# A gated mix of a state-space convolution and linear attention: two small steps that may run on either engine, and a newly written-out order

## The chip, the cores and the metric

The kernel runs on one core of a Trainium2 chip. The metric is device time in microseconds of one execution, the median of repeated runs. The seven runs of the kernel before lie between 300.56 and 304.86 us; their median is 302.23 us. The engines that matter here are TensorE (PE in the profile; its weight loads are PEld), VectorE (DVE), ScalarE (ACT) and SyncE (SP), whose instruction queue issues nearly all data transfers (DMAs). GpSimd (POOL) does a few small fills.

## What is computed

The input `x` is 2048 positions of 512 channels in bf16. One branch is a state-space convolution, the other linear attention, and a gate mixes them:

```
g = sigmoid((x * gate_w).sum(-1))
# branch a: state-space convolution, N = 128 states per channel
dt = exp(log_dt);  logdA = dt * (A_re + 1j*A_im);  dB = dt * (B_re + 1j*B_im)
P  = exp(logdA[:, :, None] * l)            # l = 0 .. 2047
K  = einsum("dn,dnl,dn->dl", C, P, dB).real
y  = irfft(rfft(pad(x)) * rfft(pad(K)));   a = y + x * Dskip
# branch b: linear attention, 32 heads of 16
q, k, v = split(xb @ wqkv)                 # xb: the kernel is given x for it
phi(t) = [softmax(t @ w_phi), softmax(-t @ w_phi)]
kv = phi(k)^T v;  z = sum(phi(k));  o = phi(q) kv / (phi(q) z + 1e-6);  b = o @ wo
out = g * a + (1 - g) * b
```

(The reference calls both branches with the same `x`.)

## The kernel before, in words

**Stages.** The start loads `x` as `UD` (four DMAs `ud0` to `ud3` of 512 KB, one per 128 channels, L287 and L1412), builds trigonometric tables for the Fourier steps, and turns the six parameter matrices into the small tables `Ctab` and `Dtab` (prepare, L261). For that it needs `log_dt` in two shapes, `ldc` (1 KB) and `ld` (128 KB), loaded together by one step, `load_ld` (L284, L1408). `ldc` feeds `dtc = exp(ldc)` on ScalarE (L403), which two VectorE products read (L412); `ld` feeds `exp(ld)` (L429). Meanwhile TensorE transforms `x` (psA at L582 into `XAu`, psB at L226 into `XU`), which goes to DRAM as `XUd`. Then come the keys (`pk`, `Ek`, `Zk`, `vr`, `kvp`) and the queries (`pq`, `Eq`, `bps`).

Woven in between are eight groups h = 0 to 7 of 64 channels for the convolution kernel `K` (kgen, L991). Each has two chunks c = 0, 1. For a chunk, ScalarE writes a table `E` (two exponentials) and a table `cs` (cosine and sine), VectorE multiplies them (r_neg L1010, r_pos L1013) and changes the sign of one quarter of the result, `R[:, 1, 0]` (L1014). VectorE also makes `A` (two products at L1005, in groups 4 to 7 a sum at L1018). TensorE multiplies `A` by the table (kps, L213). Sines and exponentials lie in different ScalarE tables, so the sines come in batches of four chunks between two table loads. Four groups of 128, 128, 128 and 64 channels run through `transform` (psB, the product with `U` at L1139, psz, a trip through DRAM as `Zd`, psy). The gate product `o` or `ZA` (ou, L1205) reads psy and is stored. The last 64 channels take `finish` (L1217), which stays on the chip.

Most results of TensorE are copied out of PSUM by `evict` (L554), a step that may run on ScalarE (`nc.scalar.copy`, L563) or on VectorE (`nc.vector.tensor_copy`, L561).

**The order is written out by hand.** Every step is a node added to `Plan` (L92) with an engine, a cost in us and its dependencies. `Plan.run` takes the nodes in the order of the string `ORDER` (two digits per node, base 64), takes the engine of each free step from `SIDES` (0 or 1) and the PSUM pool from `RINGS`. The costs and the `move` value of a DMA are only notes that the order was made with; nothing at run time reads them. What they change is the order. Each engine runs its own instructions strictly in that order: a step that waits holds up all behind it on its engine. SyncE's queue issues the DMAs in that order too.

Tiles are scarce: four `E`, four `cs` and three `A` buffers, one `KD`, two pools of PSUM of two tiles each for this work. A step that takes one waits for the last reader of the buffer's earlier use.

Of the kernel before, what the change touches and what calls it, by code (L numbers as in the profile page):

```python
# [10 lines left out]
ACT = mybir.ActivationFunctionType  # L11
ALU = mybir.AluOpType
# [79 lines left out]
class Plan:  # L92
# [3 lines left out]
    ORDER = ("000n0L0O0M0P0Q0R0N0-0_100S0T0U0k0l0h0105110206080e0i0V0W1217180X131419151a0Y0Z0m161b1c03040j1v1r1u1d1j0o1q1k1l0p1x1e1f"  # L96
             "1w1g1N0b0c091R0v0a0f070y0g0d2E2G1Q1s1m1n1t1h1T2I1M1A2K2F1P1z1B1C1F2J1O2H2M2O2Q2L2N1D1E1G2P2S2T1H1I2R2U2W2V2Y2X1J2-301L"
             "1W1U312_2Z1S3234331y1V1X361Y351Z38393a3b3c3d3e3g3f3h3i3k1i3j1K1-1_20213l3m3n22232824293o3q3p2a25370w0x3r3s3u0q0r2y2c2b"
             "262g3t3w3v2d2e2h2i2f3x3y0s0t3z0u2B3A3C2C2j2k2l3D3Q3R0z2p2m2q2r3B1o1p2o272t2n2v0C2s0D0E2u0F3E0G0H0A0B3F0I0J3S3T0K3G2z2A"
             "2w2x4647452D4c4f484d4g3K3L3H3I3J3N3O3P494e4r3M4u4j4h4s4i3U643V4n4v4k4o4p8S3Y4l4t4w8T8U3Z3W4y428W8V433X3_9U9V404x4C984D"  # L100
             "4z4A4m4E4q4a994G4J4B8X4H4F4b8Y4V4K8Z4I4L9da34N4W4Y4O4M444Z4P8-4X4R508_4-4S92934T9a94909b4Q9f955455914U5896519g979u4_9C"
             "529c9e599D569p5b5f535j9E9n5a9h5c9F5k575g9i5d5e5n5o5q9q9j9k9l9m5h5u9W9G5i9v5l5m9I9o5r9H5v5y5z5C9r5p5s5F9s5t5D5w5A9J5x5E"
             "9t5B5R5G5H9K5U5S5T5V5W5I5J5N9w5K5L5Y5O5P9x605Z5X9y9O61a49P5-9L5M9z5Q5_62639QaY9M9R9N9S65669A679TaZ9B686a696b6cbgbh6daW"
             "6e6f6g9X9Yb19ZaXa56h6j6la66i6k6ma76n6o9-9_bobpa03-a1a8a26W6pah6q6Yaia9a-aeapaqbbb2a_6r6s6tar6uaa6v6Zb0bq6Xab6-b3bcafbr"
             "b4ag70b56w6x6_b9b66y71baaj6z6Aacb76C6Bb8bebsbt6D6Ead72736Fasbdat6G6H74bf6K75bubv7677bibj6L78ak6McI6I6JcJ797a6Nalaubw7b"
             "6ObxambA7fbBancOcKcPcLcQcM6Q6P7c7dbGbC7g7hao7e7j6R7k7lbycRbH7ibD6Sbz6TbE7n7o6Ubk7zbmbl6V7BbFbnav7Aaw7p7DbJaxbIbRcSbSay"
             "d07CbKazbL7E7m7F7GcN7q41d6aAaDbTbUcZcT7HcU7rbM7IbV7J7K7L7tc0bNbWbXbO7M7N7Oc-d3c_cb7P7Q7U7v7Vc1bP7R7S7s7u7x7w7Wd4d5aBaC"
             "cc8cbY7yaEc3d7bZb-8db_c2bQc48ec57T7Y8f8g8h8icVcWc6dvdw8j8k7Zdxcec77X8l8081d1cXcf8m8n8ocd8pcgc8cY7-7_d2d8d9chcidadcdbex"
             "aFey8283aMaNdddy8q8rdJdzdAc9dKdedfcj8485dgdhcaez86dG8sdidjdk88dldBckeDeE8a8t8x8y8z8uaO8v8w8B8AeF87cldHdIdL8FdM8CaPaQdC"
             "898Ddm8bdRdSdDdN8G8HdEcmcne08E8IcpdqdOdUdTcodVdPdFdQdW8JdrdXe1eA8KdYeBe2eOdZePd-d_dncqcrds8Le38N8PeGdo8Me48Qe58OeCeHdt"  # L110
             "eI8RaGaJeJaKaHaIe6eKdpfjfkaLfmfnfre7eZe8eLeMe9eNe-e_dueQeafueRf0foaReSeTf1f2cscvebflfveefsctfteffDecedcweUcucxf3aSeVcy"
             "fEfFfpegfqf4fwfxfyf5fzfBfAeWfGfCfHfIfOfJfLaTeXczeYcDf6f7ehekelemcEaUaVfMfKfNeiejfPfQf8fbencFf9fRfSfTfVeoepfUcAfafWfcfd"
             "cGcHeqercBcCesfXfYfeeteuevffewfZf-fgfhf_g0fig1")
    SIDES = ("0010101010000101100000001100000000100101110100000011000000101000001101110000101001100010100100000100001010000001000000"
             "0000001010111")
    RINGS = ("0111001010110010010000000000000000100022222222222222222222222222222222000002222222222222222222222222222222200000000000"
             "00000000000000000000300000000000000000000000300000000000003000000030300000000330333033")
# [143 lines left out]
def prepare(P, tc, nc, g, evict, psum):  # L261
# [24 lines left out]
    for dj in range(4):  # L286
        P.dma(0.7 if dj < 2 else 3.0, 2.0, lambda dj=dj: g.load_ud(dj), rw=("", f"ud{dj}"), move=2.75)  # L287
# [237 lines left out]
    kp = []  # L525
    for h in range(2):
        box = Bag()
# [284 lines left out]
def queries_and_convolution(P, tc, nc, g, psum, sh, sp, sl, kv, bank, evict):  # L812
# [171 lines left out]
    lastk = []  # L984
# [6 lines left out]
    def kgen(h, T, XA, new):  # L991
# [5 lines left out]
        for cc in range(2):  # L997
# [14 lines left out]
            def r_pos(c=c, cc=cc):  # L1012
                nc.vector.tensor_tensor(out=c.R[:, :, 1], in0=T.E[cc][:, :, 32:64].unsqueeze(1).to_broadcast([128, 2, 32, 32]), in1=c.R[:, :, 1], op=ALU.mult)  # L1013
                nc.vector.tensor_scalar(out=c.R[:, 1, 0], in0=c.R[:, 1, 0], scalar1=-1.0, scalar2=None, op0=ALU.mult)  # L1014
                T.E[cc] = T.cs[cc] = None

# [11 lines left out]
            r1 = P.add("DVE", 1.65, r_pos, [r0], drop=["E"])  # L1028
# [11 lines left out]
            kps.append(P.add("PE", 2.3 if split else 1.15, kp, w + [a0, a1, r0, r1] + T.nc + T.nE + kps + lastk, take=([psq] if cc == 0 and not sep else []) + (["KD"] if cc == 0 else []),  # L1040
# [54 lines left out]
    def transform(XA, ready, Q, off, nd):  # L1095
# [83 lines left out]
        for j0 in range(0, 16, nj):  # L1179
# [21 lines left out]
            def ou(j0=j0, box=box, ok=ok):  # L1201
                gb = g.gT[:, j0:j0 + nj]
                if not ok:
                    box.o = g.fpool.tile([128, nj, nd], BF16, name="o", tag="o", bufs=3)
                nc.vector.tensor_tensor(out=box.o[:], in0=box.ps[:], in1=gb.unsqueeze(2).to_broadcast([128, nj, nd]), op=ALU.mult)  # L1205
                box.ps = None
# [7 lines left out]
            o = P.add("DVE", 1.22, ou, [y], drop=["psum"])  # L1214
# [326 lines left out]
```

## Time and profile before

| | us |
|---|---|
| median of seven runs | 302.23 (300.56 to 304.86) |
| the profiled execution, whole | 302.23 |
| its span, first to last instruction | 300.4 |
| VectorE busy (366 instructions) | 254.6 (85%) |
| ScalarE busy (302) | 226.1 (75%) |
| TensorE matmul busy (4700) | 220.8 (73%) |
| one product of 128x2048 bf16 on VectorE (L1010, L1013, L1005) | 1.22 |
| sign change, 128x1024 bf16 on VectorE (L1014), 16 times | 0.421 |
| copy 128x1024 f32 from PSUM: ScalarE / VectorE | 1.02 / 1.22 |
| copy 128x512 f32 from PSUM: ScalarE / VectorE | 0.59 to 0.63 / 0.685 |
| gate product 128x1024 on VectorE (L1205) | 1.22 |
| ScalarE exponential or sine, 128x1024 f32 | 1.05 |
| ScalarE, 128x128 f32 (Ln and Exp of `Zk`) | 0.31 to 0.34 |
| ScalarE table load, 11 times | 1.28 each |

The profiled execution is 1.8 us longer than its span: the span runs from the first instruction to the last. In the groups a line is read as: source line, engine, operation, output<-input, shapes, count | busy us, mean ns | idle time of the engine just before these instructions and what ended it. In the order of time (the timeline) a line is: start, duration, engine, line, operation, tiles, and in brackets the idle time before it with its releaser.

### The profile page before, as it was taken

To read this page: it belongs to the slowest core of one execution; us is meant where nothing else is said; L and a number is where in the kernel's file an instruction comes from. 1 tells how busy PE (TensorE), PEld (TensorE's weight loads), DVE (VectorE), ACT (ScalarE), POOL (GpSimd) and SP (SyncE) were. 2 spreads that over 40 slices of the span, in tenths; PEclk is the share of its full clock that TensorE was granted. 3 is DMA by queue.
4 is the path that set the end of the run, shared out by engine and by line. 5 is a ranking of instruction groups with operands and counts; after the bars stand their busy time and mean duration, and the time that the engine had idled before them with its cause. 6 is when DMAs were issued, how large, how long until landed. Compare 5 with 4: busy or idle time off the path is not lost.

```text
span 300.4 us, 10490 instructions
## 1 busy us (share of the span) xinstructions
PE 220.8 (73%) x4700; PEld 132.2 (44%) x4700; DVE 254.6 (85%) x366; ACT 226.1 (75%) x302; POOL 4.6 (2%) x17
## 2 busy tenths in 40 slices
PE   0005666444998698985999789999879999689780
PEld 0005554344343264543356554555544445455560
DVE  7786889997599999998997999999989589886541
ACT  2966989998799999989997889874758885742000
POOL 4000000000000000001000000000000000000000
PEclk9999959975799999998699999999979999999796
DMA  5998788679794000000034216475555693849634
GB/s 105 140 161 134 176 118 132 177 126 384 241 366 149 0 4 2 4 3 4 0 82 145 103 51 175 129 190 179 158 147 138 198 258 72 227 128 244 124 63 71
DMA packets 71452, 39.88 MB, mean 133 GB/s; under 512 B 57200, under 2 KB 63472, under 8 KB 71408
## 3 DMA queue, kind: packets, MB, share of 16 engines
q1 hardware_dynamic: 70352, 38.96, 53.2%
q8 instruction: 36, 0.59, 0.8%
q10 hardware_dynamic: 1056, 0.26, 0.5%
q14 instruction: 8, 0.07, 0.1%
HBM read 24.53 MB, written 14.94 MB: 131 GB/s over the span
## 4 chain that ended last, share of the span: by engine, by line
PE 33%; DVE 25%; ACT 20%; issue 4%; DMA 1%; SPq 1%; ACTq 0%; DVEq 0%
PE bps L963 7%; ACT cs L83 5%; PE kps L213 4%; DVE A L1005 4%; PE pk L700 3%; ACT E L83 2%; PE psz L1151 2%; PE psz L1286 2%; PE psB L1123 2%; ACT Ek L83 2%; DVE cs L1013 2%; ACT XA L563 2%; DVE cs L1010 2%; PE pq L887 2%; DVE Ua L1139 1%
## 5 line engine op out<-in xcount | busy, mean ns | idle before, releaser
L1005 DVE TENSOR_TENSOR A<-Ctab,Dtab 128x2048 bf16<-128x2048 bf16 x32 | 38.7, 1219 | 0.1
L582 PE MATMUL psA<-W,UD 128*64 128x256 bf16 x128 | 12.9, 356 | 27.8 <-DMA UD<-in_A_u_dram 26.0
L83 ACT ACTIVATE E<-args 128x1024 bf16<-128x1024 f32 x32 | 31.1, 1047 | 0.5 <-PE args L778 0.4
L83 ACT ACTIVATE cs<-args 128x1024 bf16<-128x1024 f32 x32 | 30.6, 1049 | 0.0
L963 PE MATMUL bps<-Mw,Eq 128*128 128x512 bf16 x128 | 30.4, 380 | 0.0
L213 PE MATMUL kps<-cs,A 128*32 128x64 bf16 x1536 | 25.9, 224 | 4.4 <-ACT cs L83 1.1
L213 PEld LDWEIGHTS <-A 128*32 128x32 bf16 x1536 | 24.5, 152 | 9.2 <-issue 5.4
L582 PEld LDWEIGHTS <-UD 128*64 128x64 bf16 x128 | 11.2, 203 | 29.3 <-issue 29.3
L1010 DVE TENSOR_TENSOR cs<-E,cs 128x2048 bf16<-128x2048 bf16 x16 | 19.5, 1219 | 2.1 <-ACT cs L83 2.1
L712 DVE TENSOR_REDUCE Zk<-Ek 128x64 f32<-128x1024 bf16 x16 | 18.8, 1211 | 2.3 <-ACT Ek L83 2.3
L1013 DVE TENSOR_TENSOR cs<-E,cs 128x2048 bf16<-128x2048 bf16 x16 | 19.5, 1219 | 0.1
L83 ACT ACTIVATE Ek<-pk 128x512 bf16<-128x512 f32 x32 | 17.2, 610 | 2.3 <-PE pk L700 2.3
L226 PE MATMUL psB<-XAu,TB 64*128 64x128 bf16 x256 | 11.1, 248 | 10.7 <-ACT XU L563 4.1
L963 PEld LDWEIGHTS <-Eq 128*128 128x128 bf16 x128 | 11.5, 97 | 15.7 <-issue 3.4
L700 PE MATMUL pk<-Wkp,xT 128*128 128x512 bf16 x64 | 17.8, 421 | 0.0
L83 ACT ACTIVATE Eq<-pq 128x512 bf16<-128x512 f32 x32 | 16.5, 608 | 1.0 <-PE pq L887 1.0
L732 PE MATMUL vp<-Wv,xT 128*128 128x512 bf16 x64 | 15.8, 380 | 1.1 <-DVE vb L561 1.1
L887 PE MATMUL pq<-xT,Wqp 128*128 128x512 bf16 x64 | 15.9, 382 | 0.0
L226 PEld LDWEIGHTS <-TB 64*128 64x128 bf16 x256 | 9.6, 110 | 12.0 <-issue 10.4
L75 ACT ACT_TABLE_LOAD x11 | 14.1, 1283 | 0.9 <-PEq L1525 0.7
L563 ACT CAST XAu<-psA 128x1024 bf16<-128x1024 f32 x10 | 9.6, 1017 | 4.2 <-PE psA L582 4.2
L1068 PE MATMUL psA<-W,KD 128*128 128x256 bf16 x64 | 10.3, 294 | 2.9 <-ACT cs L83 2.2
(197 smaller groups left out, 476.2 us busy)
## 6 DMA issues: line engine op xcount, KB each, us to landing
XUd<-XUd SPq DMA_DIRECT2D x8, 512.0 KB
Ua<-XUd SPq DMA_DIRECT2D x8, 512.0 KB
Ub<-XUd SPq DMA_DIRECT2D x8, 512.0 KB
aexp<-apd SPq DMA_DIRECT2D x16, 256.0 KB
XUd<-XU SPq DMA_DIRECT2D x8, 384.0 KB
ZB<-Zd SPq DMA_DIRECT2D x10, 256.0 KB
Zd<-Ra SPq DMA_DIRECT2D x9, 256.0 KB
UD<-in_A_u_dram SPq DMA_DIRECT2D x4, 512.0 KB
```

Source lines behind the costliest of these rows:

```text
L83: i = self.nc.scalar.activation(**kw)
L213: nc.tensor.matmul(kps[32 * dj:32 * dj + 32, g4, e, :].rearrange("p (o t) -> p o t", o=2), lhsT=A[q][:, o, :, :, d].rearrange("p a b -> p ...
L226: nc.tensor.matmul(ps[:, e, sl, :], lhsT=fc.TB[rows, r, 1 - ri:3 - ri, :].rearrange("p a b -> p (a b)"), rhs=XA[rows, r, ri, :], start=(ri ...
L582: nc.tensor.matmul(box.ps[64 * e:64 * e + 64, i, :], lhsT=g.UD[:].rearrange("p t (e g) -> p g e t", e=2)[:, gw * h + 4 * g4 + i, e, :], rh ...
L700: nc.tensor.matmul(box.ps[:], lhsT=g.xT[st // 4][:, kt, ss], rhs=g.Wkp[:, kt, :], start=(kt == 0), stop=(kt == 3))
L712: nc.vector.tensor_reduce(out=K.Z[:, u, :, :], in_=K.E[:, u, :, :].rearrange("p g (h f) -> p g h f", f=16), axis=mybir.AxisListType.X, op= ...
L732: nc.tensor.matmul(box.ps[:], lhsT=g.xT[st // 4][:, kt, ss], rhs=g.Wv[:, kt, :], start=(kt == 0), stop=(kt == 3))
L887: nc.tensor.matmul(box.ps[:], lhsT=g.Wqp[:, kt, 128 * m:128 * m + 128], rhs=g.xT[b][:, kt, :], start=(kt == 0), stop=(kt == 3))
L963: nc.tensor.matmul(box.ps[:], lhsT=Q.e[m][:, sg, 128 * i:128 * i + 128], rhs=g.Mw[:, 4 * sg + m, :], start=(k == 0), stop=False, skip_grou ...
L1005: nc.vector.tensor_tensor(out=c.A[q][:].rearrange("p o a b d -> p (o a) b d"), in0=Ct.to_broadcast([128, 8, 8, 32]), in1=Dt.to_broadcast([ ...
L1010: nc.vector.tensor_tensor(out=c.R[:, :, 0], in0=T.E[cc][:, :, 0:32].unsqueeze(1).to_broadcast([128, 2, 32, 32]), in1=c.R[:, :, 1, :, ::-1] ...
L1013: nc.vector.tensor_tensor(out=c.R[:, :, 1], in0=T.E[cc][:, :, 32:64].unsqueeze(1).to_broadcast([128, 2, 32, 32]), in1=c.R[:, :, 1], op=ALU ...
```

## The change

Four things change in the code, and the order with them.

1. The sign change is cut out of `r_pos` into a node of its own, `r_sign`, after `r_neg`, on VectorE or ScalarE. The kps step waits for it too.
2. The gate product of `transform` may run on ScalarE, as one instruction for each 128-wide (or 64-wide) position, with the gate as a per-partition scale.
3. The `move` note of the four `ud` loads is 3.7 instead of 2.75.
4. `ORDER`, `SIDES` and `RINGS` are new.

```diff
-    ORDER = ("000n0L0O0M0P0Q0R0N0-0_100S0T0U0k0l0h0105110206080e0i0V0W1217180X131419151a0Y0Z0m161b1c03040j1v1r1u1d1j0o1q1k1l0p1x1e1f"
...
+    ORDER = ("0L0k0h0i000n0M0O080_0j0e0f0N01040o0-0y090p0l0m0a0P0Q0R10110S0U0V0W0X0T0Y1213170Z14151819161a1b0g05020b030c0d06072E2G1u"
...
-        P.dma(0.7 if dj < 2 else 3.0, 2.0, lambda dj=dj: g.load_ud(dj), rw=("", f"ud{dj}"), move=2.75)
+        P.dma(0.7 if dj < 2 else 3.0, 2.0, lambda dj=dj: g.load_ud(dj), rw=("", f"ud{dj}"), move=3.7)
...
             def r_pos(c=c, cc=cc):
                 nc.vector.tensor_tensor(out=c.R[:, :, 1], in0=T.E[cc][:, :, 32:64].unsqueeze(1).to_broadcast([128, 2, 32, 32]), in1=c.R[:, :, 1], op=ALU.mult)
-                nc.vector.tensor_scalar(out=c.R[:, 1, 0], in0=c.R[:, 1, 0], scalar1=-1.0, scalar2=None, op0=ALU.mult)
                 T.E[cc] = T.cs[cc] = None
+
+            def r_sign(c=c):
+                if c.n.at == "DVE":
+                    nc.vector.tensor_scalar(out=c.R[:, 1, 0], in0=c.R[:, 1, 0], scalar1=-1.0, scalar2=None, op0=ALU.mult)
+                else:
+                    nc.scalar.activation(out=c.R[:, 1, 0], in_=c.R[:, 1, 0], func=ACT.Copy, scale=-1.0)
...
-            r1 = P.add("DVE", 1.65, r_pos, [r0], drop=["E"])
+            r1 = P.add("DVE", 1.22, r_pos, [r0], drop=["E"])
+            rs = c.n = P.add([("DVE", 0.43), ("ACT", 0.97)], 0.43, r_sign, [r0])
...
-                nc.vector.tensor_tensor(out=box.o[:], in0=box.ps[:], in1=gb.unsqueeze(2).to_broadcast([128, nj, nd]), op=ALU.mult)
+                if box.n.at == "DVE":
+                    nc.vector.tensor_tensor(out=box.o[:], in0=box.ps[:], in1=gb.unsqueeze(2).to_broadcast([128, nj, nd]), op=ALU.mult)
+                else:
+                    for j in range(nj):
+                        nc.scalar.activation(out=box.o[:, j], in_=box.ps[:, j], func=ACT.Copy, scale=gb[:, j:j + 1])
...
-            o = P.add("DVE", 1.22, ou, [y], drop=["psum"])
+            o = box.n = P.add([("DVE", 1.22), ("ACT", 2.6 if nd == 128 else 4.4)], 1.22, ou, [y], drop=["psum"])
```

Read out of the strings, the new order and sides are these.

- **Sides.** Sign changes go to ScalarE for (h, c) = (1,1), (3,0), (4,1), (5,0), (7,0), the other eleven stay. Gate products go to ScalarE for the first half of channels 128 to 255 and of channels 256 to 383 (eight instructions of 128x128 each). Of the evictions, 29 move from ScalarE to VectorE (20 of 128x1024, nine of 128x512) and 23 from VectorE to ScalarE (16 and seven). One small copy, `ti2` (two instructions of 128x128), goes to ScalarE. Without the sign changes, by stage: in the start VectorE takes two 128x1024 more on balance; with the keys one 128x1024 more and two 128x512 fewer; from the end of the keys to the last sum of `A` two 128x1024 and two 128x512 more. After that sum it takes two 128x512 more, and one 128x1024, two gate products and `ti2` fewer.
- **SP at the start.** Before: the six turned parameter loads, `ud0`, `load_ld`, `ud1`, `ud3`, `ud2`, `wTq`, the two `pz` writes, the small weights with `Wv`, `wTk`, then the `xT` loads. New: the six, `ud1`, `ud3`, `ud0`, `load_ld`, `ud2`, the small weights with `Wv`, `wTq`, a `pz` write, and the `xT` loads ahead of `wTk`. ScalarE issues its two parameter loads before its first sine instead of after it.
- **VectorE at the start.** Three parameter products that need no `log_dt`, then the products of L412 that do, as before. New: the third product with `nAim` and the two steps at L444 and L445 come ahead of the first eviction of `XAu`; evictions 0, 1, 2 of `XAu` are on VectorE, 3 to 7 on ScalarE (before they alternate); `attention_consts` (L231) comes before the first turn of trigonometry instead of within it.
- **Into the keys.** Before: ScalarE's last copy (`Wkp`), table load, gate exponential, then the first `Ek`. New: table load and the first two `Ek` directly, the gate exponential later.
- **Groups 6 and 7.** Before: the four `E` tables of groups 6 and 7 (G12 to G15) are all made while the products `bps` of the third query block (b = 2) run, and ScalarE loads the sine table after its last copy of that block. New: G12 and G13 are made during b = 1, G14 and G15 at the start of b = 2, and the sine table is loaded before ScalarE copies the third `bps` of that block; the argument product of the last chunk comes before kps of group 6 instead of after it. After the last copy of `bS` VectorE has, up to the last sum of `A`: before, r_pos, two products, r_neg, r_pos, a product, r_neg, two products with `U`, a sum, r_pos, a product, a sum; new, r_pos, two products, a sum, r_pos, two products, two products with `U`, a sum.
- **The end.** In `finish` the second copy of `Xb`/`Xa` is on ScalarE instead of VectorE. The last store-bound psy of channels 256 to 383 comes on TensorE before the second inverse step (L1286) instead of after it. The two copies of `KD` of group 7 are on VectorE.

## The prediction

> **What bounds the kernel now.** I read the busy shares first (VectorE 85%, ScalarE 75%, TensorE 73%), then the chain of waits, which goes through all of them (TensorE 33% of the span, VectorE 25%, ScalarE 20%): no engine alone is the bound. So I asked for the stretches between events of the start, the keys, the queries, the last `bps` and the last sum of `A`. Columns: stretch, length, busy of PE, PEld, DVE, ACT, POOL, clock, DMA share, GB/s.
>
> ```profile
> 27.14:267.69 240.55, 198.20 (x3907) 116.62 (x3904) 219.29 (x294) 205.22 (x278) 1.11 (x2) 0.93 0.49 133
> 27.14:75.30 48.16, 28.03 (x473) 24.36 (x470) 43.27 (x82) 43.82 (x48) 0.16 (x1) 0.80 0.79 180
> 75.30:142.00 66.70, 57.49 (x1272) 29.51 (x1270) 61.80 (x84) 63.35 (x99) 0.95 (x1) 0.96 0.26 86
> 142.00:224.00 82.00, 74.74 (x1468) 42.48 (x1466) 77.15 (x90) 66.40 (x98) 0.00 (x0) 0.94 0.41 121
> 224.00:250.20 26.20, 24.17 (x276) 11.78 (x276) 21.03 (x23) 19.92 (x22) 0.00 (x0) 1.00 0.78 202
> 250.20:267.69 17.49, 13.78 (x424) 8.49 (x423) 16.04 (x17) 11.73 (x14) 0.00 (x0) 1.00 0.53 140
> ```
>
> From the first eviction to the last sum of `A` VectorE idles 240.55 - 219.29 = 21.3 us. With the keys both VectorE and ScalarE are full (93% and 95%), from 142 to 224 VectorE is (94%), from 224 to 250 TensorE (92%), and from 250 to 268 VectorE again (92%). The gaps that matter are single waits, found in VectorE's timeline:
>
> ```profile
> 27.14 1.22 DVE L561 CAST XAu<-psA 128x1024 bf16<-128x1024 f32 x1 [2.90 <-PE psA L582]
> ...
> 240.19 1.23 DVE L561 CAST Xb<-psB 128x1024 bf16<-128x1024 f32 x1 [2.82 <-PE psB L1123]
> ...
> 246.74 1.22 DVE L1010 TENSOR_TENSOR cs<-E,cs 128x2048 bf16<-128x2048 bf16 x1 [0.70 <-ACT cs L83]
> ...
> 259.28 1.22 DVE L1010 TENSOR_TENSOR cs<-E,cs 128x2048 bf16<-128x2048 bf16 x1 [1.38 <-ACT cs L83]
> ```
>
> Last, the transfers of the start: the SP timeline, and the stretches of one microsecond around them.
>
> ```profile
> 8.55 0.75 SPq L1412 DMA_DIRECT2D UD<-in_A_u_dram  x1
> 9.35 1.52 SPq L1408 DMA_DIRECT2D ldc<-in_A_log_dt_dram  x1
> 10.91 0.49 SPq L1409 DMA_DIRECT2D ld<-in_A_log_dt_dram  x1
> 11.45 7.61 SPq L1412 DMA_DIRECT2D UD<-in_A_u_dram  x3
> ```
>
> ```profile
> 11.00:12.00 1.00, 0.00 (x0) 0.00 (x0) 0.96 (x2) 1.00 (x1) 0.00 (x0) 1.00 1.36 218
> 12.00:13.00 1.00, 0.00 (x0) 0.00 (x0) 0.18 (x1) 1.00 (x2) 0.00 (x0) 1.00 1.39 138
> 13.00:14.00 1.00, 0.00 (x0) 0.00 (x0) 0.80 (x2) 1.00 (x2) 0.00 (x0) 1.00 1.01 87
> 14.00:15.00 1.00, 0.00 (x0) 0.00 (x0) 0.66 (x2) 1.00 (x2) 0.00 (x0) 1.00 0.92 182
> ```
>
> The rate falls to 87 GB/s at 13 to 14 us and is back at 182 after. I read the dip as `ldc`'s tiny pieces, passing after `ud0` and before the other three.
>
> **The change part by part.** First the work, by durations of the groups. VectorE's evictions: (20 - 16) x 1.22 + (9 - 7) x 0.685 = +6.3 us. Two gate products less, 2 x 1.22 = -2.4; `ti2` -0.4; five sign changes, 5 x 0.421 = -2.1. Sum +1.3 us. ScalarE: (16 - 20) x 1.02 + (7 - 9) x 0.6 = -5.3, `ti2` +0.6, five signs at about 1.0 (a 128x1024 exponential takes 1.05; ends 0.9 and 1.05) = +5.0, two gate products of eight instructions each. An operation of 128x128 took 0.31 to 0.34 us, and neighbours overlap by about 0.1 (two exponentials of 128x512, 0.61 each, took 1.08): 8 x 0.22 to 8 x 0.34, 1.8 to 2.7, taken as 2.5 for their PSUM reads and strided use, so +5.0. Sum +5.3. Both engines together do 6.6 us more work.
>
> The Trainium skill, "ScalarE: Activation LUTs", Rules for kernel authors, speaks against the change: multiply on VectorE, up to about three times faster in bf16. The rows agree for the sign (0.421 against some 1.0). By the page's estimate, "What ACT_TABLE_LOAD costs", 186 ns + 0.833 ns an element, a sign is 1.04 us, and the sum is the same. The same page, "Table sets", puts copy into every set, so that no table load is added; no run here shows `ACT.Copy` in an ACTIVATE.
>
> *Start to keys.* `load_ld` now stands behind three `ud` loads instead of one. In this trace the four `ud` and `ld` pass from about 10 us to 25.7, with the dip at 12.8 to 14.3, so the last three take (25.7 - 14.3) / 3 = 3.8 each. Behind three, `ldc` lands at 25.7 - 3.8 = 21.9 or so; if transfers don't keep their order, at the old time. The table load ends at 17.3, so `dtc` slips from 17.3 to 22, and VectorE, whose queue has the product of L412 next, stands from about 17.4 to 22.1: 4.7 us. What waits behind it is everything to the first eviction: 412, 415, 416 and the other parameter products, then L444 and L445, about 8.0 us by the strides in the timeline, to 30.2. The first eviction starts there, not at 27.14. It isn't a loss of the full 3 us: the old order had waits of 2.90 here, and 1.2 and 1.1 us near 34 and 41, and had the product with `nAim` and L444, L445 (1.75 us) still to do. Walking both queues on with the old durations, ScalarE's evictions of `XAu` end at 38.5 (old 33.7), the first turn of trigonometry on VectorE at 47.4 (old 50.0, but with six more evictions done and `attention_consts`, 2.2 us, and one copy not done), ScalarE's last copy before the keys near 73.2 plus 1 for waits (old 74.2). There the new order gains: before, the table load ended at 75.5 and the first `Ek` began at 77.0, behind the gate exponential and `pk`; now `pk` runs under the table load, and `Ek` begins near 75.5. Value -1.5 us; ends -5 (`ldc` not late: VectorE's queue is through L445 at 25.5 and free for the first eviction at 27.1, so `XAu` ends some 3.4 earlier than walked, plus the 1.5) and +3.2 (the 4.7 stays, less the 1.5).
>
> *Keys.* ScalarE +1.0 (sign) + 2 x 0.6 - 1.0, VectorE +1.22 - 1.37 - 0.42: half of the sum, as both are full: +0.3, ends -0.6 and +1.2.
>
> *Queries to the last sum.* VectorE: 2 x 1.22 + 2 x 0.685 - 4 x 0.421 = +2.1. Against that, the waits shown at 240, 246.7 and 259.3, together 4.9 us, fall where the old order had sines of groups 6 and 7 not ready. They now come some copies earlier, and the products that read them are queued at that place. After the last `bS` copy VectorE had 17.5 us to the last sum; of the new list ten products at 1.13 (their stride) are 11.3. The difference has to fit before, where TensorE is the bound and VectorE idled 5.2 us. I take 4.2 of the 4.9, as the waits for TensorE itself (0.24 and 0.63) stay and something new will be late: the `bps` chain. Value -2.1; ends -2.8 and +2.1 (nothing recovered).
>
> *After the last sum.* `Xb`'s copy and the product beside it now run on two engines: -1.2 (VectorE's copy lay between two products). The psy put ahead of the second L1286 costs TensorE 1.0 on the path. The two `KD` copies stand behind a gate product on VectorE, 0.1. Value -0.1; ends -1.2 and +1.2. The ScalarE gate products lie where it idles (2.7 and later 27 us free); without that cover each costs 1.3.
>
> Sum: -1.5 + 0.3 - 2.1 - 0.1 = -3.4. The profiled execution is 302.23 whole, equal to the median of the runs, so about **298.8 us**.
>
> The order of passing is also in the skill, "DMA: Bandwidth & Descriptors", Queues, rings and completion order: an engine takes a ring's descriptors in ring order. By it `ldc` is late, which the dip also says.
>
> **The rivals.**
> *The waits move, and the work stays (slower).* Up to the last sum VectorE gets 2.44 (start) - 0.57 (keys) + 2.13 = 4.0 us more work. If it idles 21.3 us there as before, the end comes 4.0 - 0.1 later: 306.1. For it: two of three stretches are over 92% full, and a reordered queue of strict order makes new waits. Against: 4.9 us of the idle time sits in three waits whose cause is moved. It decides from the point where VectorE's idle time between first eviction and last sum stays at about 21 us.
> *The late `ldc` is paid in full (no change).* Then +3.2 instead of -1.5: 302.23 + 3.2 + 0.3 - 2.1 - 0.1 = 303.5. For it: ScalarE's first `Dtab` exponentials wait as well, and from 44 to 74 both engines had few gaps to catch up in.
> *`ldc` isn't late (faster still).* -5 in the start: 295.3. Against it stands the dip.
> *The signs on ScalarE hold up kps.* r_sign follows in ScalarE's queue, and kps waits for it now. Behind r_sign stand the sines or copies, 1 us each. A sign taken at the wrong time is one wait of about 1 us on TensorE; five make +2, 300.8 with the rest as above.
>
> **How the numbers follow.** A difference of under 1%, 3.0 us, is about what a measurement of this kernel can't tell from none. Forecast with the waits filled (about 296 to 299.2) 0.33, `ldc` in time 0.08: faster 0.41. `ldc` paid in full, or signs that hold up, or half of each: 0.27 within 1%. Work stays: 0.32 slower. The likeliest sum is 298.8. The range for 8 in 10 takes the early `ldc` (295.3) with a little, and the slower case with some of the late `ldc` on top: 294.8 to 307.5. That leaves out both ends added up.
>
> **What would show it.** Right: the first `Ek` at 76 or earlier; `dtc` at 21 to 23 and VectorE idle for over 4 us before L412; the three shown waits gone and VectorE's idle time to the last sum near 17 to 18; the last sum to the end about as long as before (32.7 us). Signs at 0.9 to 1.05 and gate instructions at 0.2 to 0.35 on ScalarE, still eleven table loads. Wrong: `dtc` at 17 (the transfer step falls), VectorE idle of 21 or more (the filling falls), or new waits of TensorE on a sign.

## The result, and the profile after

The changed kernel is slower: 306.14 us median (301.69 to 310.45, 27 runs) against 301.93 for the kernel before (299.06 to 306.54, 64 runs). The ratio is 1.0096, with a 95% interval of 1.0071 to 1.0121. It is taken over the faster executions of each kernel alone (for the changed one 15 of 28, those within 1.5% of its fastest), which is why it is smaller than the 1.4% between the medians. The forecast was 298.8 us, faster: the range of 294.8 to 307.5 holds the time, but the sign is wrong. The profiled execution of after took 304.52 us whole, 302.7 in its span, against 302.23 and 300.4 of before.

The events of the prediction (first `Ek`, first step after the keys at L825, last sum of `A`) cut both executions alike. First the stretches of before, then those of after, the whole way from the first eviction and the three between the events. The columns are the prediction's.

```profile
76.99:136.40 59.41, 53.35 (x1253) 27.73 (x1252) 56.58 (x65) 57.28 (x91) 0.48 (x1) 0.98 0.28 91
136.40:267.69 131.29, 115.13 (x2179) 63.93 (x2178) 118.88 (x145) 103.65 (x139) 0.47 (x1) 0.96 0.48 134
267.69:300.40 32.71, 21.45 (x786) 14.38 (x784) 15.73 (x16) 3.37 (x4) 0.00 (x0) 0.86 0.57 124
```

```profile
29.67:267.95 238.28, 196.37 (x3813) 116.25 (x3813) 221.65 (x293) 205.85 (x286) 1.11 (x2) 0.94 0.47 130
74.94:136.06 61.12, 53.72 (x1252) 28.09 (x1251) 57.66 (x66) 58.71 (x95) 0.95 (x1) 0.99 0.26 88
136.06:267.95 131.89, 112.87 (x2111) 63.59 (x2110) 120.51 (x145) 104.86 (x145) 0.00 (x0) 0.95 0.49 137
267.95:302.70 34.75, 22.95 (x856) 15.21 (x854) 13.35 (x12) 7.13 (x13) 0.00 (x0) 0.88 0.60 131
```

Length against length: the start -2.05 us (the first `Ek` at 74.94, not 76.99), the keys +1.71, the queries up to the last sum +0.60, what follows +2.04. Together +2.30 of the span; the prediction had -1.5, +0.3, -2.1 and -0.1.

Each of these lengths is that of one execution. The traces of the experiments below, where a part of the order is new in some and old in others, show what repeats. The first `Ek` comes at 74.8 to 75.7 us with the new start (76.9 to 77.8 with the old), the keys take 61.1 to 62.1 us (59.4 to 60.2), and what follows the last sum takes 34.4 to 37.7 with the change's end (31.5 to 33.9). The queries vary most: 128.8 to 132.3 (130.7 to 133.1).

VectorE's idle time from the first eviction to the last sum is 238.28 - 221.65 = 16.6 us, not 21.3. So the waits were filled, as forecast, and still the last sum stands where it was (267.95 and 267.69). VectorE's timeline shows the parts; the bracket is the idle time before the line and its releaser:

```profile
21.39 0.69 DVE L412 SCALAR_TENSOR_TENSOR pt<-Aim,dtc 128x512 f32<-128x512 bf16 x1 [4.09 <-ACT dtc L83]
...
29.67 1.22 DVE L561 CAST XAu<-psA 128x1024 bf16<-128x1024 f32 x1
...
166.61 1.23 DVE L561 CAST Xa<-psB 128x1024 bf16<-128x1024 f32 x1 [2.37 <-PE psB L1129]
...
243.84 1.23 DVE L561 CAST Ra<-psz 128x1024 bf16<-128x1024 f32 x1 [0.82 <-PE psz L1157]
...
254.18 1.23 DVE L1010 TENSOR_TENSOR cs<-E,cs 128x2048 bf16<-128x2048 bf16 x1 [1.45 <-ACT cs L83]
```

`dtc` is late and the first eviction comes at 29.67, which answers to 27.14. Two of the three shown waits (2.82 at 240, 0.70 at 246.7) are gone; the third is still there, 1.45 us at 254.18. And one is longer than its like in before: at 166.61 VectorE waits 2.37 us for TensorE, where the nearest wait of before, in its own timeline, is

```profile
165.80 1.23 DVE L561 CAST XA<-psA 128x1024 bf16<-128x1024 f32 x1 [1.73 <-PE psA L1068]
```

TensorE's timeline of after ahead of that place:

```profile
155.66 0.23 PE L906 MATMUL zs<-Eq,SSw 128*32 128x128 bf16 x3
157.65 0.27 PE L906 MATMUL zs<-Eq,SSw 128*32 128x128 bf16 x5 [1.77 <-issue]
...
157.94 1.87 PE L213 MATMUL kps<-cs,A 128*32 128x64 bf16 x111
161.38 0.45 PE L213 MATMUL kps<-cs,A 128*32 128x64 bf16 x17 [1.57 <-issue]
161.77 4.22 PE L887 MATMUL pq<-xT,Wqp 128*128 128x512 bf16 x12
```

Eight `zs` matmuls are broken after three, 128 `kps` matmuls after 111, and nothing that the profile shows was waited for ("issue"). Between the two ends of these stops lie 256 instructions, matmuls and weight loads together. The trace has 36 packets of 16,384 bytes on TensorE's instruction queue, 64 bytes for each of 256 instructions. Two of them were fetched at 155.24 (landed 156.19) and at 158.75 (landed 159.86), and TensorE went on 1.5 us after each landing. So these are waits for code. In before the same two blocks came at 155.89 and 160.53, and its TensorE timeline has both `kps` whole:

```profile
157.65 2.12 PE L213 MATMUL kps<-cs,A 128*32 128x64 bf16 x128
...
161.86 2.18 PE L213 MATMUL kps<-cs,A 128*32 128x64 bf16 x128
```

The kernel before isn't free of such stops: it has 1.14 us at 218.82, 1.44 at 262.40 and 1.81 at 293.82, 4.4 us in all. After has 7.9, and the difference is about these two.

The stretches of one microsecond, with the granted clock, the DMA share and GB/s as the last three columns:

```profile
154.00:155.00 1.00, 1.00 (x48) 0.63 (x40) 1.00 (x2) 0.94 (x2) 0.00 (x0) 1.00 1.17 401
156.00:157.00 1.00, 0.00 (x0) 0.00 (x0) 1.00 (x3) 1.00 (x2) 0.00 (x0) 1.00 0.88 338
160.00:161.00 1.00, 0.00 (x0) 0.00 (x0) 0.61 (x2) 0.32 (x1) 0.00 (x0) 0.50 0.00 0
163.00:164.00 1.00, 1.00 (x4) 0.43 (x3) 1.00 (x2) 0.31 (x1) 0.00 (x0) 0.50 0.11 21
```

The first stop falls into a burst of transfers (401 GB/s, share over 1). The second doesn't, but the clock has halved by then, and TensorE does its next 12 matmuls at 0.35 us a piece (0.23 for 12 at 149.02, at full clock). The burst is in SP's queue:

```profile
148.30 0.33 SPq L1167 DMA_DIRECT2D Zd<-Ra  x1
148.75 0.35 SPq L1120 DMA_DIRECT2D Ua<-XUd  x1
149.14 1.19 SPq L644 DMA_DIRECT2D XUd<-XUd  x2
152.68 0.33 SPq L1120 DMA_DIRECT2D Ub<-XUd  x1
154.31 0.32 SPq L1167 DMA_DIRECT2D Zd<-Ra  x1
```

The two `XUd` copies of L644 (the mirrored half of channels 256 to 383) stood on SP at 76 to 82 us before, in a row with the other six. The new order moves them between the loads of `Ua`, `Ub` and `Zd`. After the two stops TensorE starts the first `bps` at 181.78 (before 177.33), 4.5 us behind, and begins the last short matmuls of `bps` at 254.79 (250.55).

### The profile page after: what moved, and what is told of

Same layout as the page of the kernel before. It is cut to its first block, busy times and chain, and to the rows that moved or that the text cites. A ratio compares the mean times of both kernels' runs of the same rounds, so it can differ in the third digit from the quotient of the medians.

```text
span 302.7 us, 10516 instructions
## 1 busy us (share of the span) xinstructions
PE 223.0 (74%) x4700; PEld 134.9 (45%) x4700; DVE 256.0 (85%) x363; ACT 229.9 (76%) x319; POOL 4.6 (2%) x17
## 4 chain that ended last, share of the span: by engine, by line
ACT 32%; PE 27%; DVE 25%; issue 5%; DMA 4%; SPq 4%; DVEq 0%; ACTq 0%
ACT E L83 6%; ACT cs L83 6%; PE kps L213 4%; PE bps L963 4%; PE pq L887 4%; ACT Ek L83 4%; DVE A L1005 3%; SPq L293 2%; DMA ldc<-in_A_log_dt_dram 2%; PE psz L1157 2%; PE psB L1129 2%; ACT XA L563 2%; ACT L75 2%; SPq L1422 2%; PE psz L1296 2%
## 5 line engine op out<-in xcount | busy, mean ns | idle before, releaser
L712 DVE TENSOR_REDUCE Zk<-Ek 128x64 f32<-128x1024 bf16 x16 | 19.1, 1212 | 2.1 <-ACT Ek L83 2.1
L226 PE MATMUL psB<-XAu,TB 64*128 64x128 bf16 x256 | 13.2, 274 | 5.6 <-DVE XU L561 2.6
L887 PE MATMUL pq<-xT,Wqp 128*128 128x512 bf16 x64 | 16.8, 407 | 0.0
L563 ACT CAST XA<-psA 128x1024 bf16<-128x1024 f32 x12 | 12.1, 1018 | 3.4 <-PE psA L1074 3.4
L226 PEld LDWEIGHTS <-TB 64*128 64x128 bf16 x256 | 11.4, 124 | 7.4 <-issue 7.2
L796 PE MATMUL args<-selE,stat 64*128 64x512 bf16 x32 | 9.5, 376 | 5.8 <-ACT cs L83 3.8
```

Source lines behind the costliest of these rows:

```text
L226: nc.tensor.matmul(ps[:, e, sl, :], lhsT=fc.TB[rows, r, 1 - ri:3 - ri, :].rearrange("p a b -> p (a b)"), rhs=XA[rows, r, ri, :], start=(ri ...
L563: nc.scalar.copy(out=o, in_=i)
L712: nc.vector.tensor_reduce(out=K.Z[:, u, :, :], in_=K.E[:, u, :, :].rearrange("p g (h f) -> p g h f", f=16), axis=mybir.AxisListType.X, op= ...
L887: nc.tensor.matmul(box.ps[:], lhsT=g.Wqp[:, kt, 128 * m:128 * m + 128], rhs=g.xT[b][:, kt, :], start=(kt == 0), stop=(kt == 3))
```

## The experiments

The theory: the copies moved on SP cause the first stop, and the stops eat what the filled waits gave. Against it stood three others: that the loss is the late `ldc`, the moved work (signs and gates on ScalarE), or the order of the end. Two digits of the strings name a step; `3_` is the pair of copies of L644, `02` `load_ld`, `b9` the second half of a kps. All ratios are to the kernel before, with 95% intervals.

### The stops

**The copies back early (e1), and late in the kernel before (e2).**

```diff
- bn3_b7
+ bnb7
- 429n
+ 423_9n
```

> The changed kernel, with one step moved back on SyncE's queue: the two copies within DRAM that mirror XUd for channels 256 to 383 (L644) are issued with the other six, near 85 us, and not at 149 us beside Ua, Ub and a Zd write. Theory 'late code': in the changed kernel these transfers hold up the loading of TensorE's instructions; that is what the two stops of 1.77 and 1.57 us at 155.9 and 159.8 us with no wait are, and the clock of 0.50 from 158 to 164.7 us follows from them. Then the first stop is gone, the second is under 0.7 us, the clock between 155 and 166 us stays at 0.9 or more, the first bps of query block 0 starts near 178 us instead of 181.8, and the time falls by 2.5 to 5 us: ratio to the kernel before 0.993 to 1.001. Rival 'dense code': two kps and two rows of zs in a run simply use up instructions faster than they are loaded; then both stops stay within 0.5 us and the ratio stays at 1.007 to 1.012. Rival 'the work is the bound' (VectorE and ScalarE carry 6.6 us more work): the stops go, but the end moves by less than 1 us, ratio 1.006 to 1.012.

```diff
- 433X3_9U9V404x4C
+ 433X9U9V4x4C
- a9a-aeapaq
+ a9a-ae3_4041apaq
```

> The kernel before, with that one step moved as the change moves it: the mirror copies of XUd for channels 256 to 383 (L644) are issued behind the third load of Ua/Ub, near 155 us, all else in the old order. Theory 'late code': TensorE stops without a wait for 1 to 2 us at least once between 155 and 168 us and its clock falls to 0.50 after it; 1 to 5 us slower, ratio 1.003 to 1.016. Rival 'dense code': in the old order there is always a sparse stretch (pq, psz) between the dense ones, so no stop, ratio 0.998 to 1.002.

e1: 1.0061 [1.0024, 1.0097]. e2: 1.0036 [0.9997, 1.0075]. TensorE's timeline of e1, then of e2:

```profile
157.68 0.27 PE L906 MATMUL zs<-Eq,SSw 128*32 128x128 bf16 x5 [0.56 <-issue]
161.14 0.43 PE L213 MATMUL kps<-cs,A 128*32 128x64 bf16 x17 [1.26 <-issue]
```

```profile
164.38 1.11 PE L213 MATMUL kps<-cs,A 128*32 128x64 bf16 x61 [1.19 <-issue]
```

With the copies away the first stop is 1.2 us shorter, and the clock stays at 1.00 from 158 to 165 (0.52 in after). TensorE goes on at the same time in both, though (157.65 and 157.68): it came to that place 1.2 us later in e1, 0.74 of them because the keys ended later. Moved into the old order the copies make a stop where there was none; the clock stays at 1.00 there. And the second stop stays in e1: it has another cause.

**Fewer small matmuls in a row (e5; alone, with the copies left late, e16).** The second half of that kps goes behind a `pq`, in e5 on top of e1:

```diff
- b5b8b9afagbp6W6q6Y6-
+ b5b8afagbp6W6q6Yb96-
```

> The changed kernel, with the mirror copies of XUd early (as in e1_mirror_early) and, besides, the second kps product of group 2 behind two pq of query block 1 instead of ahead of them, so that between kps, zs and kps on TensorE there are now sixteen-instruction products. In e1 the two stops of TensorE went from 1.77 and 1.57 us to 0.56 and 1.26 us. Theory 'both, late and dense': the rest of the stops is the dense run of small products, so both fall under 0.3 us now; the exponentials Eq of block 1 start 2 us earlier, the first bps of block 0 at about 178 us (177.3 in the kernel before, 181.8 in the changed one, 180.0 in e1), ratio to the kernel before 0.996 to 1.003. Rival 'the work is the bound': the stops go, bps still starts at 180 or later, since VectorE's and ScalarE's queues hold it, and the ratio stays at 1.004 to 1.009.

> The changed kernel, with the second kps of group 2 behind two pq (as in e5_spread) and the mirror copies of XUd late, as the change has them. Stops of TensorE between 155 and 164 us: 3.34 us in the changed kernel, 1.82 in e1 (copies early), 0.6 to 0.8 in e5 (both). If the dense run is the cause: under 1 us, ratio 1.003 to 1.006. If the copies are: 1.5 to 2 us stay in the first stop, ratio 1.006 to 1.010. If both add up: about 2 us, ratio 1.006 to 1.008.

e5: 1.0037 [1.0001, 1.0074]. e16: 1.0074 [1.0016, 1.0131]. Timeline of e5, then of e16:

```profile
158.19 0.27 PE L906 MATMUL zs<-Eq,SSw 128*32 128x128 bf16 x5 [0.56 <-issue]
...
160.45 2.30 PE L213 MATMUL kps<-cs,A 128*32 128x64 bf16 x128
```

```profile
159.64 0.27 PE L906 MATMUL zs<-Eq,SSw 128*32 128x128 bf16 x5 [1.75 <-issue]
...
161.90 2.30 PE L213 MATMUL kps<-cs,A 128*32 128x64 bf16 x128
```

The two edits act apart: the early copies take away most of the first stop, the spread the second, in whichever company. The other traces agree: the first stop is 1.15 to 2.53 us in the six with late copies, at most 0.95 in the seven with early ones; the second is 1.03 to 1.64 in seven without the spread, and none of the six with it has one there. In time only both edits together are certain: after less e5 is 0.59 ± 0.44% (half-widths added as squares), 1.8 us. The stretches of e5:

```profile
137.29:266.30 129.01, 109.82 (x2091) 63.28 (x2109) 120.28 (x144) 104.66 (x145) 0.00 (x0) 0.96 0.48 132
266.30:301.60 35.30, 22.99 (x852) 15.45 (x856) 13.44 (x13) 7.30 (x14) 0.00 (x0) 0.93 0.60 129
```

The queries up to the last sum take 129.01 us, 2.28 less than before: the prediction's -2.1, once the stops are gone (128.8 to 129.4 in e1, e5, e7 and e18). The end keeps +2.59.

The half clock is no fixed part of the loss. e3 below has late copies and no spread, as after has; its TensorE timeline, and the stretch behind the first stop:

```profile
156.90 0.27 PE L906 MATMUL zs<-Eq,SSw 128*32 128x128 bf16 x5 [1.15 <-issue]
...
160.63 0.43 PE L213 MATMUL kps<-cs,A 128*32 128x64 bf16 x17 [1.64 <-issue]
```

```profile
158.00:165.00 7.00, 5.36 (x135) 3.41 (x128) 4.58 (x8) 3.97 (x9) 0.00 (x0) 1.00 0.05 13
```

With both stops at full clock its queries are about 1.5 us shorter than before (from L825 at 135.84 to the last sum at 265.67). Of the 2 us between that and after's +0.60, 0.55 are shorter stops; much of the rest may be the half clock. Single executions don't give a firm price for it: e16 has one of the stops, at full clock, and its queries take 131.5 us.

### The late `ldc`

**`ldc` early in after (e3), late in before (e4).**

```diff
- 0O080_
+ 0O08020_
- 0g05020b
+ 0g050b
```

> The changed kernel, with load_ld put back behind one load of UD instead of three. dtc should come at about 17 us instead of 21.2, VectorE's 4.1 us before L412 go, and the first eviction of XAu start near 26 to 27.5 us instead of 29.7. Theory 'given back with the keys': the changed kernel already reached the keys 2.05 us earlier than the old one and kept 0.3 of it at their end, so another gain at the start is lost there too, and the end moves by less than 1 us: ratio 1.005 to 1.012. Rival 'on the path' (the prediction's ends): first Ek 2 to 3.5 us earlier, and the end with it, ratio 0.998 to 1.003.

```diff
- 05110206080e0i
+ 051106080e020i
```

> The kernel before, with load_ld put behind three loads of UD instead of one, all else in the old order: the price of the late ldc alone. dtc near 22 us instead of 17.3, the first Ek later than 77.0. Paid in full it is the prediction's 3.2 us, ratio 1.010; if the old order's waits near 28, 34 and 41 us take it up, under 1 us, ratio 1.000 to 1.003.

e3: 1.0080 [1.0037, 1.0122], level with after. Its first eviction comes at 27.41, 2.26 us earlier, but the first `Ek` at 74.77, only 0.17 earlier: VectorE gives the gain back in a wait that after doesn't have,

```profile
41.08 0.43 DVE L454 TENSOR_SCALAR pt<-pt 128x512 f32<-128x512 f32 x1 [2.29 <-DMA pz<-pt]
```

e4: 1.0065 [1.0025, 1.0105], the first `Ek` 0.76 later. So in the new order the late `ldc` costs nothing that shows (after less e3 is 0.16 ± 0.49%); in the old one it would cost some 0.65%. The late `ldc` isn't the loss.

### The work

**Signs and gates back on VectorE in after (e8); the signs alone, on top of e5 (e17).** Only the sides change; e8's, of which e17 keeps the gate products on ScalarE:

```diff
- 111000010110101011010000011010000101000001001100
- 100000011000010000000000011010100011
+ 111000010010101011010000011000000101000000000100
+ 000000011000000000000000001010100011
```

> The changed kernel with its order as it is, but all five sign changes and both gate products on VectorE again, at the same places: the moved work alone. It takes 9.5 us off ScalarE and puts 4.1 us on VectorE (5 times 0.34 and 2 times 1.22). Theory 'the order costs, not the work': within 1 us of the changed kernel, ratio 1.006 to 1.013. Rival 'the work stays' (the prediction's): VectorE's 4.1 us come on the path, 1.5 to 4 us slower, ratio 1.014 to 1.023. Rival 'signs hold up kps on ScalarE': 1 to 2 us faster, ratio 1.002 to 1.006.

> e5_spread with the five sign changes on VectorE again, the gate products still on ScalarE: 5.3 us less on ScalarE, 1.7 us more on VectorE. If VectorE is what the new order waits for, 1 to 2 us slower than e5 (1.0037): 1.006 to 1.011. If the signs stand in the way of sines and exponentials on ScalarE as in the old order (e12 against e15), faster: 0.998 to 1.002. If neither, 1.002 to 1.006.

**The old order with five signs and two gate products on ScalarE (e12), and with the gate products alone (e15).** Both have the code of the change with the old sequence. The cut shows e12's sides against those of before; the places are not aligned, since signs and gate products are now choices too:

```diff
- 1101110000101001100010100100000100001010000001000000
+ 1101110000000110100110001000001010010000010001001010
```

> The old order, with the same five sign changes and two gate products on ScalarE, each in its place in the order, and nothing else changed: the moved work alone. If VectorE's 4.1 us less work (5 times 0.34 and 2 times 1.22) come off the path as far as its gaps let them: ratio 0.988 to 0.997. If ScalarE's queue, 95% busy with the keys, and waits of kps on signs eat it up: 0.998 to 1.004. If kps waits a full sign each time: 1.004 to 1.010.

> The old order, with the two gate products alone on ScalarE (eight instructions each), the sign changes on VectorE. They come behind the last sum of A, where ScalarE has little to do. If the sign changes on ScalarE are what cost in e12_work_alone (1.0086), by standing ahead of sines and exponentials in a queue that is full: ratio 0.994 to 1.002. If the gate products cost (2.2 us in place of 1.2 on the way to the stores): 1.003 to 1.009.

e8: 1.0190 [1.0094, 1.0285], which rests on two executions. e17: 1.0113 [1.0059, 1.0167], 0.76 ± 0.65% above e5. e12: 1.0086 [1.0049, 1.0123]. e15: 1.0031 [0.9995, 1.0067]. The same work helps in the new order and hurts in the old. The clearest delay there stands in e12's ScalarE timeline, and then in its VectorE timeline:

```profile
256.05 1.06 ACT L1020 ACTIVATE cs<-cs 128x1024 bf16<-128x1024 bf16 x1 [0.66 <-DVE cs L1010]
...
259.71 1.96 ACT L83 ACTIVATE cs<-args 128x1024 bf16<-128x1024 f32 x2
```

```profile
261.70 1.23 DVE L1010 TENSOR_TENSOR cs<-E,cs 128x2048 bf16<-128x2048 bf16 x1 [3.30 <-ACT cs L83]
```

The sign waits for VectorE's product and stands in the strict queue ahead of the copies and sines, so the sines of the last group start at 259.71 instead of 257.27, and VectorE's wait of 1.38 becomes 3.30. In after those sines come at 252.21, a sign ahead of them at 250.68 included. So the move of the work isn't the loss of this change; it needs the new order.

### Where in the order

**Old and new halves joined (e9 to e11, e13, e14).** Each cut shows the seam. e9: new up to the end of the keys, then old. e10: the reverse. Both have the early copies.

```diff
- 9D9R9W659E9F66679_a068
+ 9D9R9W654340449-b0669E679X
```

> The changed kernel's code with its new order and sides up to the end of the keys (L825), and from there the old order and sides (all five sign changes and both gate products of that part on VectorE); the mirror copies of XUd early, as in the old order. If the change loses its time behind the keys (late code, new waits at 238 to 243 us, the tail): ratio 0.995 to 1.001, zj (L825) near 136 us and the rest as long as before, 164 us. If the new start and keys cost time by themselves: 1.004 or more.

```diff
- 9Q9V62639C9D9R9W659E9F6667
+ 9Q5_62639Ub09Q9V9R9W65a-a_9E9F6667
```

> The other half: the old order and sides up to the end of the keys, with the early mirror copies and four signs fewer to place, and from there the changed kernel's order and sides. If the loss lies behind the keys, ratio 1.003 to 1.009 (what e1_mirror_early and e5_spread left), TensorE's stops behind 155 us 5 us in sum or more, against 4.4 in the kernel before. If it lies in the start and the keys, 0.996 to 1.001.

e9: 1.0016 [0.9974, 1.0058]. e10: 1.0085 [1.0047, 1.0123]. The start's gain and the keys' loss cancel within the interval; what is lost is lost behind the keys.

e11: new up to the last copy of `bS`, then the old end. e13: e5's order up to the denominators of the last query block, then old. e14: old up to there, then new.

```diff
- 8Q8RelfcaKemfKfdaLaMePfxeW
+ 8QePeW8RaKaNeXaOaLaMeYfxfy
```

> The changed kernel up to the last copy of bS (256 us), and from there the old order and sides: the second copies of Xb/Xa and both gate products on VectorE, the KD copies of group 7 on ScalarE, psy of channels 256 to 383 behind the second inverse step. If the order of the tail costs the 2.1 us that the last sum of A to the end grew by: ratio 1.001 to 1.006, last sum to end 33 to 34 us. If the tail only takes over TensorE's lag of 4.2 us at the last bps: 1.008 to 1.013.

```diff
- 8pd6dgaScr8q8r
+ 8p44dgdIdJd67-
```

> The changed kernel's order and sides, with the two repairs of e5_spread (early mirror copies, second kps of group 2 behind two pq), up to the last denominators of query block 3 (about 223 us); from there the old order and sides. If the new order of groups 6 and 7 and the tail holds what e5 left (1.0037): 0.996 to 1.001. If the loss that is left lies between the keys and 223 us: 1.003 to 1.007.

```diff
- 8m8n8ocl8pcocgd67-
+ 8m8n8ocl8paJdqdrds
```

> The other half: the old order and sides up to the last denominators of query block 3, then the changed kernel's. No stops at 155 to 162 us. If the new order of groups 6 and 7 and the tail costs: 1.003 to 1.008. If it does what the prediction expected of it (4.2 of 4.9 us of waits filled): 0.990 to 0.997. If neither: 0.998 to 1.002.

e11: 1.0119 [1.0069, 1.0169]. e13: 1.0093 [1.0057, 1.0129]. The old end on the new base is no better than the new end: e11, which keeps both stops, is level with after (1.0096), and e13, which doesn't, lies above e5 (1.0037). In e11's trace the end takes 32.4 us again, as before, but the last sum comes at 269.74, 1.8 us later than in after. That is its second expectation: the end takes over TensorE's lag, 4.2 us at the last `bps`. So the +2.04 of the end isn't the end's order alone. e14: 1.0431 [1.0387, 1.0476]; its halves don't fit (VectorE waits 7.11 us for a `psy` at 226.94), so it prices nothing.

### The end

**The end reordered (e6), with e5 (e7), and e5 with the psy of channels 256 to 383 back behind the second inverse (e18).** e6 puts a sign and the sum of group 7 earlier and kps ahead of the products with `U`:

```diff
- f2f5cAcDfDfffgcE
- ocHfTfIaVf6fhaWf7f8f_fEfMfNfF
+ f2fIf5cAcDfDffcE
+ ocHfTfEfMfNfFfOfgaVf6f7fPfRfQfSaWfhfif8f_
```

> The changed kernel, with the order of the last 35 us alone altered: the sum of the last chunk's A comes ahead of the two products with U, both kps of group 7 ahead of psy and of the psz that read those products, the KD copies, psA and the XA copies of group 7 ahead of the second psz, and the last psy of channels 256 to 383 behind two fill products less. Theory 'the end hangs on kps of group 7': in the changed kernel the second of them started at 271.13 us (before 268.54), since the psz of channels 384 to 447 stand ahead of it on TensorE; now it starts near 267, the first L1296 near 277 to 278.5 instead of 281.4, and the time falls by 2 to 4 us: ratio 0.996 to 1.003. Rival 'another chain ends last' (the round trip of Z through DRAM, or the stores): L1296 earlier, the end by less than 1 us, ratio 1.006 to 1.011.

> e5_spread and e6_tail together. If both theories hold and add up, 4 to 8 us off the changed kernel, ratio 0.983 to 0.996, below both kernels. If the lag of TensorE and the order of the tail are one loss seen twice, no better than the better of the two, 0.996 to 1.003. If work is the bound, over 1.002.

```diff
- g9eEeBcIgaeFgcfogbcO
+ g9eBcIgaeEgcfogbeFcO
```

> e5_spread with the last store-bound psy of channels 256 to 383 behind the second inverse step (L1296) again, and its gate product behind the second copy of Z. If that psy lies on the path, as the prediction had it: the second L1296 starts 1.0 us earlier against the first, the end 0.5 to 1.2 us earlier, ratio 0.999 to 1.002. If TensorE then only stops for code earlier or longer: 1.002 to 1.006.

e6: 1.0166 [1.0113, 1.0219]. e7: 1.0089 [1.0058, 1.0120]. e18: 1.0040 [1.0001, 1.0078]. None of them helped. In the trace e6's kps of group 7 ran at 268.46 and 271.38, hardly earlier than in after (269.12 and 271.13), and TensorE's timeline has a longer stop for code just ahead of the inverse:

```profile
284.63 0.35 PE L1200 MATMUL psy<-ZB,TJ 64*32 64x128 bf16 x12 [2.55 <-issue]
286.12 3.35 PE L1296 MATMUL psz<-TI,tN 128*32 128x64 bf16 x128
```

In e18 the second inverse begins 3.2 us after the first (280.07 and 283.28) instead of 5.0 in e5 (280.45 and 285.40; 0.74 of it is a stop for code), and the median didn't move: e18 less e5 is 0.03 ± 0.53%, 1.6 us, too coarse for the prediction's +1.0. The traces speak for the +1.0: from the first inverse to the end they take 19.1 to 20.4 us with that psy in its old place (nine traces), 20.3 to 22.8 in the new (eleven), 20.2 in e18 and 21.2 in e5, though more than the psy differs among them. Whether it is on the path stays open.

None of these versions beats the kernel before; e2, e5, e9, e15 and e18 lie within 0.4% of it.

## Why the prediction was wrong

**The step that failed: "Queries to the last sum", -2.1.** It said that of the 4.9 us in three waits 4.2 come back, with "something new" late, the `bps` chain, already in the value. It measured +0.60, 2.7 us off. The mechanism was there: two waits gone, VectorE's idle time 4.7 us less, and about the value (-2.28) in e5, where the stops are mostly gone. What the step didn't have is that the new order makes TensorE wait twice for its own code, 1.77 and 1.57 us, and that in this execution it then ran at half clock for 6.8 us. The price that the prediction put on the moved transfers was that of `load_ld` alone. The two copies of L644 move past some 70 us of SP's queue, and that was in the strings to be read; I priced every queue at the start and none in the middle. The copies and the dense run together are 0.59 ± 0.44% of the 0.96%. What is left in e5 is no gain either: against before its stretches are -1.29 (first `Ek` at 75.70), +2.18, -2.28 and +2.59, so that the keys and the end take what the start and the queries give; TensorE is still 2.4 us behind at the last `bps` (252.90 against 250.55).

**After the last sum, -0.1.** It measured +2.04, outside its ends of ±1.2. TensorE's timeline of before, then of after:

```profile
262.67 1.04 PE L1151 MATMUL psz<-Ua,TI 128*128 128x512 bf16 x4
...
268.54 1.12 PE L213 MATMUL kps<-cs,A 128*32 128x64 bf16 x64
```

```profile
267.29 1.04 PE L1157 MATMUL psz<-Ua,TI 128*128 128x512 bf16 x4
268.17 1.03 PE L1157 MATMUL psz<-Ub,TI 128*128 128x512 bf16 x4
...
271.13 1.14 PE L213 MATMUL kps<-cs,A 128*32 128x64 bf16 x64
...
295.31 0.22 PE L1323 MATMUL psy<-Z,TJ 64*32 64x32 bf16 x6 [2.44 <-issue]
```

The new list has the products with `U` just before the last sum, so the `psz` that read them stand ahead of group 7's kps on TensorE. The second half of kps starts 3.2 us after the last sum instead of 0.85. I had both lists and priced VectorE's side only. Up to the first inverse that leaves +1.1 of the +2.04 (281.44 against 280.06, less the 0.26 of the last sum); behind it the stops for code are 0.35, 0.16 and 2.44 us against 1.81 alone, 1.1 us more, about the rest. In e5 that second half starts 3.6 us after the last sum, so the stops in the queries aren't the cause of this delay. But e6, e11 and e18, which each changed a part of the end, gained nothing that the medians show. What would recover it stays open: up to 0.4%, the rest of e5, whose interval nearly holds nothing at all.

**Keys, +0.3.** Mis-sized: +1.71, above the end of +1.2. ScalarE does 1.43 us more in the stretch (forecast 1.2), VectorE 1.08 more (forecast 0.57 less), and the term took half of the sum where ScalarE, 96% full, had no room for it. No run tries this term alone. **Start, -1.5:** -2.05, right in size: `dtc` at 21.15 (forecast near 22), VectorE idle for 4.09 (4.7), first eviction 29.67 (30.2), first `Ek` 74.94 (75.5). The last step into the keys was another than written. ScalarE's timeline:

```profile
71.58 1.28 ACT L75 ACT_TABLE_LOAD   x1
74.94 1.08 ACT L83 ACTIVATE Ek<-pk 128x512 bf16<-128x512 f32 x2 [2.08 <-PE pk L700]
```

The table load ended at 72.86, not near 75.5, and `Ek` then waited 2.08 us for `pk`, which waits for VectorE's copy of `Wkp` (71.77 to 72.99). So the number owes something to luck. Together start and keys are -0.3, and e9 can't tell them from nothing.

**A slip in the sum.** By its own terms the last sum would stand at 30.2 + (219.29 + 4.0) + 17.5 = 271.0, while the stage terms put it at 267.69 - 1.5 + 0.3 - 2.1 = 264.4. For that VectorE's idle time had to be 10.9, not the 17 to 18 that the text expects. Measured: 16.6 idle, VectorE's work +2.4 instead of +4.0 (the prediction's own 1.75 us of `nAim`, L444 and L445, now ahead of the first eviction, is about the difference). Set side by side, the two sums would have shown that the forecast needed 6.6 us less idle time than the text itself expected.

**The sizes of the work** held: signs 1.04 to 1.17 (median 1.06, forecast 1.0), a gate product 2.17 for eight (forecast 2.5; one record is 0.36 to 0.42, above the 0.2 to 0.35 forecast, and they overlap), `ti2` 0.57, still eleven table loads. Over the span VectorE is busy 1.4 us more (forecast 1.3), ScalarE 3.8 (5.3). The Trainium skill's rule to multiply on VectorE and not on ScalarE ("ScalarE: Activation LUTs", Rules for kernel authors) is right for the single instruction (0.42 against 1.06, 1.22 against 2.17); e8 and e17 show that in this order the dearer place is the better one.

**The rivals.** "The waits move, and the work stays" gave 306.1, the measured median almost to the tenth, and by the wrong way: its condition was idle time of 21 us, which is 16.6. The late `ldc` as a loss is not borne out by e3, the early `ldc` is refuted by 4.09 us before L412. No kps of after waited for a sign on ScalarE.

## What to carry to other kernels

A new written-out order moves every queue. List each DMA that changes place, in the middle as at the start, with what moves beside it at its new time, and look at TensorE's runs of small matmuls there. Where a stage sum and a sum over one engine (first event, plus work, plus idle time) can both be made, make both before believing either. When work goes to the slower engine, ask what is behind it in that queue: the same five signs cost about 0.5% in one order (e12 less e15, 0.55 ± 0.5%) and saved 0.8% in the other.

## What the runs showed of the hardware

TensorE's code arrives in blocks of 256 instructions, and a run of 128 matmuls of 32 rows with their weight loads uses up a block in 2.1 us. In none of the twenty traces do the fetches of two blocks start less than 3.2 us apart; near the stops a fetch took 0.9 to 1.9 us, and TensorE went on 1.1 to 1.6 us after it landed. So such a run can stall with hardly a transfer beside it (1.26 us in e1, DMA share 0.05 from 158 to 165).

Beside transfers a stop is longer because the fetch starts late, not because it is slow. Counted from the matmul 128 places before the first stop, the fetch started after 2.18 us in after and 0.92 in e1, and then took 0.94 and 0.87 us. From 154 to 155 us the DMA moved 401 GB/s in after and 33 in e1; from 156 to 157, beside the stop itself, 338 and 354. In the six traces with late copies the fetch started after 1.4 to 2.9 us, in the seven with early ones after 0.4 to 1.3; e16 (2.35) and e5 (0.43) differ in the copies alone.

The Trainium skill, "Runtime: NRT & Kernel Launch", Instruction fetch mechanics, has the blocks of 16 KiB and 256 instructions, which agrees, and calls the crossing of a boundary mostly hidden. Of the 36 blocks of after, six show a stop of 0.3 us or more; the largest, 2.44 us, isn't hidden at all.

A stop doesn't always cost the clock. After e16's 1.75 us it stayed at 1.00 from 158 to 165, and so it did in e3, e8 and e11, which have both stops (1.15 to 1.49 and 1.37 to 1.64 us). In after, with 1.77 and then 1.57, it was 0.50 from 157.9 to 164.8 and 1.00 after that; in e6, with 2.53 and 1.62, from 159.3 to 169.5. What decides between the two wasn't tried.
